# Converting a weight matrix in column parts: the first up projection of a fused HGRN2 and feed-forward kernel

## The chip, the cores and the metric

The kernel runs on one core of a Trainium2 chip. The metric is the device time of one execution in microseconds (us), lower is better. In the profile the engines are PE (TensorE: matmuls), DVE (VectorE), ACT (ScalarE), POOL (GpSimd) and SP (SyncE, which here only issues DMAs). Each engine runs its own instructions in order, and engines wait for each other on semaphores.

## The reference

An attention block without softmax (per batch, head and step a decayed outer-product state) is followed by a feed-forward block that multiplies two projections:

```python
f = 1.0 / (1.0 + np.exp(-f_logit))            # q, k, v, f_logit: (4, 8, 768, 48)
for t in range(S):
    state = f[:, :, t, :, None] * state + np.einsum('bhd,bhe->bhde', k[:, :, t], v[:, :, t])
    y[:, :, t] = np.einsum('bhd,bhde->bhe', q[:, :, t], state)
x = y.transpose(0, 2, 1, 3).reshape(3072, 384)
a = x @ w1                                    # w1, w2: (384, 1024)
b = x @ w2
h = a * b @ w3                                # w3: (1024, 1024)
out = h @ w_out                               # w_out: (1024, 384)
```

q, k, v and f_logit come as 32-bit floats. The four weight matrices come as 64-bit floats, and the kernel converts them to 32 bits on the chip.

## The kernel before, in words

**Chunks and blocks.** The 4 x 768 steps are 24 chunks (u = 0 to 23) of 128 steps, all 8 heads together. For each chunk DVE makes the running products of the gates by two scans (L531 forward, L553 backward) and from them Q (L547) and K (L561). PE multiplies them (L586, copied to SBUF by ACT at L709), POOL masks the result (L715), and PE makes the chunk's values in one visit (L660, L679). From chunk 4 on such a visit also begins the next chunk (L586 and L692), so the visit of chunk u needs K of chunk u+1 turned. Chunk 0 to 4 are turned by four PE transposes (L600) into a PSUM bank and a copy by ACT (L756). From chunk 5 on it is done without PE: ACT splits K into 16-bit halves (L732), a transposing DMA on SP's queue moves them (L735), ACT merges them (L740). The test for it is in `turning`, L750.

The values go to DRAM (`written`, L896, SP's queue) and come back in the layout of the projections (`gathered`, L899, POOL's queue). Four chunks make a block of 512 steps for the feed-forward part.

**Feed-forward.** Block 0 uses plain products (`part`, L950): a visit `up(jc, which)` multiplies 256 steps by 128 columns jc of w1 (which = 0) or w2 (which = 1) as three matmuls over the 384 rows (L928), each of which the profile shows as two instructions. ACT copies the w1 result (L965), DVE multiplies it by the w2 result (L970). There are 8 column groups jc, and the half of a matrix is jc // 4. Later blocks use products with fewer multiplications (L1024, L1179). w3 and w_out are first multiplied into one matrix wc by PE ("folds", L1496), which is then used by the down projection (`down`).

**Conversion of the weights.** `fetch` loads raw 64-bit words into a buffer in `place`. Per load, ACT turns the low words into something that can be joined (L1432). Then three DVE instructions make 32-bit floats: `shifted` (L1447), `signed` (L1451, the last reader of the raw buffer) and `joined` (L1457). w1 and w2 are four items of 384 rows by 512 columns, called A (w1, columns 0 to 511), B (w2, the same columns), C (w1, columns 512 to 1023) and D (w2, the same). An item has three loads, and 3 x 512 = 1536 elements per partition. D's raw words go to the same place as A's.

**Order.** Nothing is ordered by hand. All work is entered into `Plan` as tasks with an engine, an estimated cost, what they depend on, and a priority. `listed` simulates the engines and takes at each step the task that can start first, by priority if several can. The tasks are then emitted in that order, which fixes the order on every engine; the semaphore waits follow from what the instructions read and write. So a changed cost or priority may move instructions anywhere in the program. DMAs are tasks of a queue and of a pretended engine with a latency (`moves`). In the first stage the DVE work is also held in a fixed order, `"23ACBD"`: the scans and products of chunks 2 and 3, then the items. Up to planned time 130 (`FULL`), gaps that the plan sees on PE are filled with matmuls on a constant tile (`idle`, L408):

```python
for t in plan.order():
    if t["eng"] == "PE" and t["at"] < FULL:
        n = int((t["at"] - ready_at) / 0.43)
        if ready_at and n:
            idle(n)
        ready_at = t["end"]
```

Of the kernel before, what the change touches and what calls it, by code (L numbers as in the profile page):

```python
# [37 lines left out]
I32 = mybir.dt.int32  # L38
U32 = mybir.dt.uint32
U16 = mybir.dt.uint16  # L40
ALU = mybir.AluOpType
# [3 lines left out]
B, H, S, D = 4, 8, 768, 48  # L45
# [11 lines left out]
UB = TB // C  # L57
# [9 lines left out]
KH = KF // 2  # L67
# [12 lines left out]
SURE_W = 2.0  # L80
SURE_K = 1.0
SURE_Z = 0.8
WITH_DMA = 1.2
NEED = (0.0, 1.0, 2.0, 3.0)
DUE = (5.0, 8.0, 24.0, 26.0)
EARLY = "23ACBD"
# [212 lines left out]
def ranged(ctx, tc, q, k, f_logit, v, w1, w2, w3, w_out, out, ident, w12, wc, left):  # L299

    nc = tc.nc
# [72 lines left out]
    plan = Plan()  # L374
# [86 lines left out]
    tk = [{} for _ in range(NU)]  # L461

    def need(u):
        return NEED[u] if u < 4 else 60 + 14.5 * (u - 4)

    def turn_of(item):

# [5 lines left out]
    def moves(n, size, rate, emit, deps, prio, late=0.0, since=0.0, lanes=("lane",), issue=0.45, eng="SP"):  # L473


        for j in range(n):
            i = plan.add(eng, issue, (lambda: None) if j else emit, [d] if j else deps, prio - j * 1e-3, takes=lanes, lag=0.85, since=since)
            d = i
            t = plan.add("DMA", size / n / rate, lambda: None, [i], prio - j * 1e-3, lag=1.1 + late, frees=[i])
        return t  # L480
# [266 lines left out]
    def turning(u):  # L747

        s, t = st[u], tk[u]
        if u > 4:  # L750
            crossing(u)
            return

        def turned():
            s["kt"] = work.tile([P, HP, R], F32, name="kt")
            nc.scalar.copy(s["kt"].rearrange("p (b two) r -> p b (two r)", two=2), s["pk"])  # L756

        if u < NPE:
            t["t"] = plan.add("PE", 0.45, lambda: turn(u), [t["k"]] + past(u, 1, "d"), need(u) - 999)
        else:  # L760
            t["t"] = plan.add("PE", 0.45, lambda: turn(u), [t["k"]], need(u) - 999, takes=["f"])
        t["e"] = plan.add(
            "ACT", 0.55, turned, [t["t"]] + past(u, 2, "s"), need(u), frees=[t["t"]] if u >= NPE else [],
        )
# [32 lines left out]
    def rest(u):  # L797
        s, t = st[u], tk[u]
        opens, closes = u % NCH == 0, u % NCH == NCH - 1
        n0 = need(u)  # L800
# [111 lines left out]
        if u < NPE:  # L912
            t["z"] = plan.add("PE", 1.6, moved, [t["y"]], n0 - 996, takes=["f"], frees=[moving])
            t["x"] = plan.add("ACT", 0.55, settled, [t["z"]] + before, n0 - 20, frees=[t["z"]])
        else:
            t["z"] = moves(2, 197, 300, written, [t["y"]], n0 - 100, 0.8)
            t["x"] = moves(1, 197, 250, gathered, [t["z"]] + before, n0 - 100, SURE_X, issue=WITH_DMA, eng="POOL")


# [13 lines left out]
    def ffn(n):  # L933
# [16 lines left out]
        def part(c0, c1, jcs):  # L950
            cols = slice(c0 * C, c1 * C)
            nt = (c1 - c0) * C
            cost = 6 * max(0.135, nt * 0.322 / 384)

            def up(jc, which):
                def emit():
                    s["pu", jc, which, c0] = bank()
                    three(
                        s["pu", jc, which, c0][:, 0:nt], [up_weights(w12, which, kc, jc) for kc in range(KM)],
                        [s["xt"][:, kc, cols] for kc in range(KM)],  # L960
                    )
                return emit

            def keep_a(jc):
                return lambda: nc.scalar.copy(a_b(jc)[:, cols], s["pu", jc, 0, c0][:, 0:nt])  # L965

            def times(jc):
                def emit():
                    ab = a_b(jc)[:, cols]
                    nc.vector.tensor_tensor(ab, s["pu", jc, 1, c0][:, 0:nt], ab, ALU.mult)  # L970
                return emit

            for jc in jcs:
                h = jc // KH
                x = [tk[n * UB + c]["x"] for c in range(c0, c1)]
                n0 = 100 * n + 50 + 10 * (jc >= KH)
                pa = plan.add("PE", cost, up(jc, 0), x + pieces[0, h], n0, takes=["f"])
                ka = takes_ab(jc, plan.add("ACT", 0.2 + nt * 0.28 / 384, keep_a(jc), [pa], -10, frees=[pa]))
                pb = plan.add("PE", cost, up(jc, 1), x + pieces[1, h] + [pa], n0 - 5, takes=["f"])
                kb = plan.add("DVE", 0.16 + nt * 0.4 / 384, times(jc), [pb, ka], -10, frees=[pb])  # L980
                s["up"] += [pa, pb]
                s["done"][place_of(jc) // KH].append(kb)
# [424 lines left out]

        return [g for a, m, gs in users if a < where + n and where < a + m for g in gs]

    def fetch(loads_, where, prio, due, dst, waits=(), deps=()):  # L1410

        total = sum(n for _, n, _ in loads_)
        if not wide:
# [27 lines left out]
        spot[0] = (a0 + (total + 511) // 512 * 512) % 2048  # L1441
        m = magnitudes[:, a0 : a0 + total]
        mine = range(a0 // 512, (a0 + total + 511) // 512)
        s = {}

        def shifted():
            nc.vector.tensor_scalar(m.bitcast(U32), hi, 3, None, ALU.logical_shift_left)  # L1447

        def signed():
            s["to"] = dst()  # L1450
            nc.vector.scalar_tensor_tensor(  # L1451
                s["to"].bitcast(U32), hi, 0x80000000, lo, ALU.bitwise_and, ALU.bitwise_or
            )

        def joined():
            to = s["to"].bitcast(I32)
            nc.vector.tensor_tensor(to, m.bitcast(I32), to, ALU.add)  # L1457

        past = [joins[i] for i in mine if i in joins]
        h = plan.add("DVE", 0.16 + 0.27 * w, shifted, landed + past, due, shared=True)  # L1460
        g = plan.add("DVE", 0.16 + 0.53 * w, signed, [*low, h] + list(waits), due)
        j = plan.add("DVE", 0.16 + 0.53 * w, joined, [h, g], due - 1, shared=True)
        parts.append((g, j))
        joins.update({i: j for i in mine})
        got.append(g)
        return [j]

    def weights():
        due = dict(zip(((0, 0), (1, 0), (0, 1), (1, 1)), DUE))
        for item in (x for x in EARLY if x in "ABCD"):  # L1470
            half, which = divmod("ABCD".index(item), 2)
            w = (w1, w2)[which]
            cols = slice(half * KH * P, (half + 1) * KH * P)
            pieces[which, half] = fetch(
                [(kc * KH * P, KH * P, w[kc * P : kc * P + P, cols].unsqueeze(1)) for kc in range(KM)],
                EARLY_AT[item], turn_of(item), due[which, half],
                lambda which=which, half=half: w12[:, which, half].rearrange("p k c -> p (k c)"),
            )

    def folding():  # L1480
# [138 lines left out]
    for u in range(NU):  # L1619
# [26 lines left out]
            judged = plan.add("DVE", 0.2, decided, [moves(1, 0.4, 250, heard, [sent], 0, SPREAD)], -20)  # L1646
        if u % UB == UB - 1:
            ffn(u // UB)
    first, last = {}, {}
    for item in EARLY:  # L1650
        if item in "ABCD":
            half, which = divmod("ABCD".index(item), 2)
            mine = pieces[which, half]
            first[item], last[item] = [j["deps"][0] for j in mine], mine
        else:
            t = tk[int(item)]
            first[item], last[item] = [t["p"]], [t["q"], t["k"]]
    for a, b in zip("1" + EARLY, EARLY):
        for t in first[b]:
            t["deps"] += last[a] if a != "1" else [tk[1]["q"], tk[1]["k"]]  # L1660
    ready_at = 0.0
    for t in plan.order():
        if t["eng"] == "PE" and t["at"] < FULL:
# [383 lines left out]
```

## Time and profile before

| what | value |
|---|---|
| median of 3 runs | 452.43 us (452.41 to 453.13) |
| profiled execution | 452.64 us, span 450.9 us |
| TensorE clock granted, mean | 0.998 |
| PE busy | 442.3 us, 98% of the span |
| DVE busy | 357.1 us, 79% |
| ACT busy | 253.6 us, 56% |
| POOL busy | 96.0 us, 21% |
| PE share of the chain that ended last | 95% |

The span is what the profiler saw from the first to the last instruction; the execution's own time has 1.7 us around it. "Busy" is time in which an engine had an instruction running; the filler matmuls count as busy. The chain is followed back from the last instruction, at each step to what released it. In rows of instructions in order of time, the first number is the start and the second the duration in us, "x8" is how many were merged, and brackets give the idle time of the engine before the row and what ended it. In rows of groups, the numbers after the bar are busy us in total and mean ns of one.

### The profile page before, as it was taken

The page shows a single profiled execution, that of the slowest core. Times are in us where ns is not written, and L with a number is a line of the kernel's source. Part 1 is how long each engine was busy: PE and PEld are TensorE (multiplying, and loading weights), DVE is VectorE, ACT ScalarE, POOL GpSimd, SP SyncE. Part 2 cuts the span into 40 slices and gives each one's busy share as a digit, 9 for nine tenths or more (in the row PEclk, how much of TensorE's full clock was granted, in tenths as well). Part 3 has the DMA queues.
Part 4 walks back from the last instruction along what each step waited for, and adds up shares of the span by engine and source line. Part 5 has one row for each costly group of instructions (what it writes and reads, how often), then busy time and mean ns, then how long its engine had stood idle before and what let it go on. Part 6 is the DMA issues. An engine that isn't in the chain of part 4 may idle for free.

```text
span 450.9 us, 11720 instructions
## 1 busy us (share of the span) xinstructions
PE 442.3 (98%) x4720; PEld 386.2 (86%) x4720; DVE 357.1 (79%) x615; ACT 253.6 (56%) x559; POOL 96.0 (21%) x132
## 2 busy tenths in 40 slices
PE   7999999999999999999999999999999999999995
PEld 6788885566899888889988889998899988889995
DVE  8999998999898978998889958965669557667541
ACT  4576245554546768676676346656666656666100
POOL 9551003133432344344333102000020000000000
PEclk9999999999999999999999999999999999999999
DMA  6998699784566786677653156563264612331111
GB/s 177 265 401 252 251 319 318 206 201 125 127 146 173 204 184 161 141 176 194 168 145 87 27 160 218 175 206 100 93 197 154 213 47 93 94 94 48 36 71 39
DMA packets 51949, 73.10 MB, mean 162 GB/s; under 512 B 22849, under 2 KB 35010, under 8 KB 50866
## 3 DMA queue, kind: packets, MB, share of 16 engines
q1 hardware_dynamic: 49202, 64.05, 48.3%
q0 software_dynamic: 2688, 8.26, 6.4%
q8 instruction: 38, 0.62, 0.6%
q14 instruction: 21, 0.17, 0.1%
HBM read 58.88 MB, written 9.04 MB: 151 GB/s over the span
## 4 chain that ended last, share of the span: by engine, by line
PE 95%; DVE 1%; SPq 1%; DMA 1%; issue 0%; POOL 0%; POOLq 0%; DVEq 0%
PE f L928 29%; PE f L1024 17%; PE l L1179 13%; PE f L1179 10%; PE f L1496 9%; PE l L928 5%; PE py L660 3%; PE pa L586 2%; PE py L679 2%; PE pa L692 2%; SPq L497 1%; PE f L408 1%; DMA ab<-in_k_dram 1%; PE l L1024 1%; DVE K L561 0%
## 5 line engine op out<-in xcount | busy, mean ns | idle before, releaser
L715 POOL TENSOR_SCALAR_AFFINE_SELECT A<-A 64x512 f32<-64x512 f32 (+1 forms) x46 | 47.7, 1037 | 45.3 <-ACT A L709 43.1
L928 PE MATMUL f<-place 128*128 128x192 f32 x240 | 42.4, 327 | 0.0
L928 PE MATMUL f<-xt,w 128*128 128x256 f32 x192 | 42.3, 380 | 0.0
L1496 PE MATMUL f<-place 128*128 128x384 f32 x128 | 42.2, 489 | 0.0
L928 PEld LDWEIGHTS f<-xt,w 128*128 128x128 f32 x192 | 36.2, 190 | 4.9
L928 PEld LDWEIGHTS f<-place 128*128 128x128 f32 x240 | 39.6, 190 | 0.2
L1024 PE MATMUL f<-xt,w 128*128 128x256 f32 x156 | 39.2, 379 | 0.0
L1496 PEld LDWEIGHTS f<-place 128*128 128x128 f32 x128 | 24.1, 190 | 16.1
L899 POOL DMA_DIRECT2D xt<-yt x22 | 16.8, 765 | 96.9 <-PE l L1179 52.3
L1024 PEld LDWEIGHTS f<-xt,w 128*128 128x128 f32 x156 | 29.6, 190 | 4.0
L531 DVE TENSOR_TENSOR_SCAN fwd<-gate,floor 112x512 f32<-112x512 f32 x24 | 30.3, 1263 | 1.0 <-ACT gate L523 0.2
L553 DVE TENSOR_TENSOR_SCAN bwd<-gate,back 112x512 f32<-112x512 f32 x24 | 29.7, 1236 | 0.7
L740 ACT COPY kt<-halves 128x896 uint16<-128x896 uint16 x19 | 22.9, 1205 | 4.7 <-DMA halves<-A 4.7
L1024 PE MATMUL f<-place 128*128 128x256 f32 x92 | 24.9, 388 | 0.0
L1432 ACT ACTIVATE place<-place 128x512 f32<-128x512 uint32 (+2 forms) x24 | 21.3, 891 | 4.8 <-DMA place<-in_w_dram 2.7
L875 ACT ACTIVATE ys<-py 112x512 f32<-112x512 f32 x22 | 13.1, 596 | 19.1 <-PE py L679 19.1
L928 PE MATMUL f<-wc,ab 128*128 128x192 f32 x128 | 23.7, 329 | 0.1
L732 ACT COPY A<-K 112x1024 uint16<-112x1024 uint16 x19 | 19.8, 1042 | 3.8 <-DVE K L561 3.8
L928 PEld LDWEIGHTS f<-wc,ab 128*128 128x128 f32 x128 | 21.2, 190 | 0.7 <-PE f L408 0.5
L523 ACT ACTIVATE gate<-f 112x512 f32<-112x512 f32 x22 | 13.9, 633 | 12.6 <-DMA f<-in_f_logit_dram 7.8
L838 POOL TENSOR_TENSOR G<-lasts,gate 112x4 f32<-112x4 f32 x20 | 9.6, 479 | 52.3 <-ACT gate L523 26.8
L515 POOL DMA_DIRECT2D vt<-in_v_dram x20 | 11.5, 575 | 40.5 <-PE py L660 35.3
(292 smaller groups left out, 1061.8 us busy)
## 6 DMA issues: line engine op xcount, KB each, us to landing
place<-in_w_dram SPq DMA_DIRECT2D x21, 512.0 KB, 6.9
A<-in_w_dram SPq DMA_DIRECT2D x19, 512.0 KB, 3.8
place<-in_w_dram SPq DMA_DIRECT2D x8, 1024.0 KB, 6.6
q<-in_q_dram SPq DMA_DIRECT2D x46, 96.0 KB, 2.9
out_dram<-o SPq DMA_DIRECT2D x23, 192.0 KB, 2.7
k<-in_k_dram SPq DMA_DIRECT2D x44, 96.0 KB, 2.8
yt<-ys SPq DMA_DIRECT2D x44, 96.0 KB, 2.9
xt<-yt POOLq DMA_DIRECT2D x22, 192.0 KB, 4.1
```

The costliest lines, as they stand in the source:

```text
L523: nc.scalar.activation(gate[u % 2][:, 0:NQ], fu, AF.Sigmoid)
L531: nc.vector.tensor_tensor_scan(s["P"], gate[u % 2][:, 0:NQ], floor, 0.0, ALU.mult, ALU.max)
L553: nc.vector.tensor_tensor_scan(s["R"][:, ::-1], gate[u % 2][:, NQ:0:-1], back[:, ::-1], 0.0, ALU.mult, ALU.max)
L715: nc.gpsimd.affine_select(out=a, in_=a, pattern=pattern, compare_op=ALU.is_ge, fill=0.0, base=0, channel_multiplier=-1,)
L732: nc.scalar.copy(apart.rearrange("p (two n) -> p two n", two=2), s["K"].bitcast(U16).rearrange("p (n two) -> p two n", two=2))
L740: nc.scalar.copy(to, halves.rearrange("p (two n) -> p two n", two=2))
L899: nc.gpsimd.dma_start(block_xt()[:, :, cols], s["yt"].rearrange("(k p) c -> p k c", p=P))
L928: nc.tensor.matmul(out_, lhsT=lhs[i], rhs=rhs[i], start=start and i == 0, stop=i == len(lhs) - 1, skip_group_check=True,)
L1024: nc.tensor.matmul(q[nm][:, which * TH : which * TH + TH], lhsT=lhs[i](which), rhs=rhs[i], start=start and which == 0 and i == 0, stop=i = ...
L1179: nc.tensor.matmul(banks[g, c][:, which * TH : which * TH + TH], lhsT=lhs, rhs=x_node(a), start=first and which == 0, stop=True, skip_grou ...
L1432: nc.scalar.activation(part_.bitcast(F32), part_, AF.Copy, bias=2.0, scale=2.0**-51)
L1496: nc.tensor.matmul(w3s["p", jc], lhsT=w3s[jc][:, kc * P : kc * P + P], rhs=wos[:, kc], start=(kc == 0), stop=(kc == KF - 1),)
```

## The change

Six things change, all in what is entered into the plan:

- `fetch` can cut the conversion of an item into column parts. A and C (`CUT`) are cut in two parts of 256 columns each: three rows of 256 elements per part, with three DVE instructions each, instead of three instructions over 1536 elements. The loads and ACT's part stay whole.
- A visit of columns jc depends on the parts up to its own columns (the first two jc of a half on the first part, the other two on both).
- The fixed order of the first stage names the parts (`TURNS`).
- The plan counts a raw buffer as read when the joins have ended, and no longer when `signed` has ended.
- Chunk 5 is turned by PE as chunks 0 to 4 are (`u > 5`).
- Three numbers of the plan: the cost of a DMA issue on POOL (1.2 to 0.8), the spacing of the chunks' priorities (14.5 to 14.0), and an added delay in the plan after the write of the values, 0.8 to 3.0 for the chunks that are not the last of their block.

```diff
-WITH_DMA = 1.2
+CUT = "AC"
+TURNS = ('2', '3', 'A0', 'A1', 'C0', 'C1', 'B', 'D')
+WITH_DMA = 0.8
...
-        return NEED[u] if u < 4 else 60 + 14.5 * (u - 4)
+        return NEED[u] if u < 4 else 60 + 14.0 * (u - 4)
...
-        if u > 4:
+        if u > 5:
             crossing(u)
...
-            t["z"] = moves(2, 197, 300, written, [t["y"]], n0 - 100, 0.8)
+            t["z"] = moves(2, 197, 300, written, [t["y"]], n0 - 100, 0.8 if u % UB == UB - 1 else 3.0)
...
-                pa = plan.add("PE", cost, up(jc, 0), x + pieces[0, h], n0, takes=["f"])
+                pa = plan.add("PE", cost, up(jc, 0), x + pieces[0, h][: jc % KH * len(pieces[0, h]) // KH + 1], n0, takes=["f"])
...
-                pb = plan.add("PE", cost, up(jc, 1), x + pieces[1, h] + [pa], n0 - 5, takes=["f"])
+                pb = plan.add("PE", cost, up(jc, 1), x + pieces[1, h][: jc % KH * len(pieces[1, h]) // KH + 1] + [pa], n0 - 5, takes=["f"])
...
+        for c in range(cuts):
+            def of(t, c=c):
+                t = t.rearrange("p (k n) -> p k n", k=len(loads_))
+                return t[:, :, c * t.shape[2] // cuts : (c + 1) * t.shape[2] // cuts] if cuts > 1 else t
...
+            at_once = due + 0.1 * c
+            h = plan.add("DVE", 0.16 + 0.27 * w / cuts, shifted, landed + past, at_once, shared=True)
+            g = low if by_act else [plan.add("DVE", 0.16 + 0.53 * w / cuts, signed, [*low, h, *waits], at_once)]
+            j = plan.add("DVE", 0.16 + 0.53 * w / cuts, joined, [h, *g, *waits], at_once - 1, shared=True)
+            parts.append((h, j))
+            ended.append(j)
...
-        got.append(g)
-        return [j]
+        got += ended
+        return ended
...
+                cuts=2 if item in CUT else 1,
```

More of the change, by code (lines that the diff above doesn't have):

```diff
@@ L1408, in holders, with fetch @@
         return [g for a, m, gs in users if a < where + n and where < a + m for g in gs]
-    def fetch(loads_, where, prio, due, dst, waits=(), deps=()):
+    def fetch(loads_, where, prio, due, dst, waits=(), deps=(), by_act=False, cuts=1):
         total = sum(n for _, n, _ in loads_)
@@ L1443, in fetch @@
         mine = range(a0 // 512, (a0 + total + 511) // 512)
[L1444 to L1457, printed above, removed]
@@ L1459, in fetch, with shifted, whole, signed @@
-        past = [joins[i] for i in mine if i in joins]
[L1460 to L1463, printed above, removed]
+        past = [joins[i] for i in mine if i in joins]
+        ended = []
+        for c in range(cuts):
+            def of(t, c=c):
+                t = t.rearrange("p (k n) -> p k n", k=len(loads_))
+                return t[:, :, c * t.shape[2] // cuts : (c + 1) * t.shape[2] // cuts] if cuts > 1 else t
+            mc = m[:, c * total // cuts : (c + 1) * total // cuts]
+            mc = mc.rearrange("p (k n) -> p k n", k=len(loads_)) if cuts > 1 else mc
+            def shifted(of=of, mc=mc):
+                nc.vector.tensor_scalar(mc.bitcast(U32), of(hi), 3, None, ALU.logical_shift_left)
+            def whole(of=of):
+                return of(lo) if by_act else of(dst().bitcast(U32))
+            def signed(of=of, whole=whole):
+                nc.vector.scalar_tensor_tensor(whole(), of(hi), 0x80000000, of(lo), ALU.bitwise_and, ALU.bitwise_or)
+            def joined(of=of, mc=mc, whole=whole):
+                nc.vector.tensor_tensor(of(dst().bitcast(I32)), mc.bitcast(I32), whole().bitcast(I32), ALU.add)
+            at_once = due + 0.1 * c
[4 more added lines that the diff above has]
+            ended.append(j)
@@ L1648, in ranged @@
             ffn(u // UB)
[L1649 to L1654, printed above, removed]
+    chain = [(tk[1]["p"], [tk[1]["q"], tk[1]["k"]])]
+    for item in TURNS:
+        if item[0] in "ABCD":
+            half, which = divmod("ABCD".index(item[0]), 2)
+            js = pieces[which, half] if len(item) == 1 else [pieces[which, half][int(item[1])]]
+            chain.append((js[0]["deps"][0], js))
         else:
             t = tk[int(item)]
[L1657 to L1660, printed above, removed]
+            chain.append((t["p"], [t["q"], t["k"]]))
+    for (_, before), (t, _) in zip(chain, chain[1:]):
+        t["deps"] += before
     ready_at = 0.0
```

## The prediction

> **What bounds the kernel now.** I read the page first (busy times, the chain that ended last), then the waits of PE, then PE in order of time, to find where PE does nothing of use.
>
> ```profile
> span 450.9 us, 11720 instructions
> ...
> PE 442.3 (98%) x4720; PEld 386.2 (86%) x4720; DVE 357.1 (79%) x615; ACT 253.6 (56%) x559; POOL 96.0 (21%) x132
> ...
> PE 95%; DVE 1%; SPq 1%; DMA 1%; issue 0%; POOL 0%; POOLq 0%; DVEq 0%
> ```
>
> PE is busy 98% of the span and makes 95% of the chain. So the time is PE's work plus what PE loses, and another engine matters only where it makes PE wait. The waits of PE up to 130 us are four (total, times, longest):
>
> ```profile
> PE f L408 <- DVE floor L431: 1.8, 1, 1.8
> PE py L600 <- DVE K L561: 0.7, 1, 0.7
> PE f L600 <- DVE K L561: 0.5, 1, 0.5
> PE pa L692 <- issue: 0.5, 1, 0.5
> ```
>
> That is not all that PE loses. Where the planner expects a gap on PE it emits fillers (L408, a constant tile multiplied into a bank that nobody reads): a filler is a wait that looks busy. PE in order of time around the first up-projection visits (L928); start and duration come first:
>
> ```profile
> 24.90 1.89 PE L408 MATMUL f<-floor 112*128 112x256 f32 x8
> 26.72 1.00 PE L660 MATMUL py<-A,vt 64*64 64x64 f32 x32
> ...
> 29.66 0.70 PE L408 MATMUL f<-floor 112*128 112x256 f32 x2
> 30.20 4.05 PE L928 MATMUL f<-xt,w 128*128 128x256 f32 x18
> ...
> 35.56 26.17 PE L928 MATMUL f<-xt,w 128*128 128x256 f32 x120
> 61.56 0.55 PE L600 MATMUL f<-ident,K 112*128 112x112 f32 x4
> 61.95 5.36 PE L928 MATMUL f<-xt,w 128*128 128x256 f32 x24
> ```
>
> Ahead of the first L928, PE fills from 24.90 to 26.72, runs the visit of chunk 2, fills again from 29.66 to 30.20, and starts. From there no wait of PE stands in the list, and 120 matmuls in 26.17 us are 0.218 us each, against 5.36/24 = 0.223 in the short group: no hidden stall. A visit is six of them, 1.31 us. The one later loss, and the end:
>
> ```profile
> 122.10 0.60 PE L408 MATMUL f<-floor 112*128 112x256 f32 x2
> 122.76 1.57 PE L928 MATMUL f<-wc,ab 128*128 128x192 f32 x8
> ...
> 444.80 1.46 PE L928 MATMUL f<-wc,place 128*128 128x192 f32 x8
> ```
>
> So from 30.20 to 446.3 PE does work that stays, but for one pair of fillers (122.76 - 122.10 = 0.66).
>
> **The cut of A and C.** DVE converts the first half of w1 (A, 24.22 to 29.62), then the second (C, from 29.96), then B from 35.40; the rows from 55.77 are a w_out piece, of exactly the size of the new parts (768 elements):
>
> ```profile
> 24.22 1.28 DVE L1447 TENSOR_SCALAR place<-place 128x1536 uint32<-128x1536 uint32 x1 [0.61 <-DMA place<-in_w_dram]
> 25.42 0.34 DVE L788 TENSOR_TENSOR A<-pa,S 112x192 f32<-112x192 f32 x1
> ...
> 26.07 1.75 DVE L1451 SCALAR_TENSOR_TENSOR w<-place 128x1536 uint32<-128x1536 uint32 x1
> 27.86 1.76 DVE L1457 CUSTOM_DVE_ANT_0 w<-place,w 128x3072 uint16<-128x3072 uint16 x1
> 29.96 0.96 DVE L1447 TENSOR_SCALAR place<-place 128x1536 uint32<-128x1536 uint32 x1 [0.34 <-DMA place<-in_w_dram]
> ...
> 35.40 0.96 DVE L1447 TENSOR_SCALAR place<-place 128x1536 uint32<-128x1536 uint32 x1
> ...
> 39.86 0.96 DVE L1447 TENSOR_SCALAR place<-place 128x1536 uint32<-128x1536 uint32 x1
> ...
> 55.77 0.55 DVE L1447 TENSOR_SCALAR place<-place 128x768 uint32<-128x768 uint32 x1
> 56.23 0.95 DVE L1451 SCALAR_TENSOR_TENSOR place<-place 128x768 uint32<-128x768 uint32 x1
> ...
> 58.09 0.42 DVE L970 TENSOR_TENSOR ab<-f,ab 128x256 f32<-128x256 f32 x1
> ```
>
> A's data land just before 24.22 (DVE sat 0.61 us for them), and the cut doesn't move that. Today A is whole at 27.86 + 1.76 = 29.62. A part of 768 elements takes 58.09 - 55.77 = 2.32 us from start to start; with the state update of chunk 2 in between (26.07 - 25.42 = 0.65) the first part, A0, is done at 24.22 + 2.32 + 0.65 = 27.2, which is 2.4 earlier. But PE works in order and is in chunk 2's visit until 29.66, so only 30.20 - 29.66 = **0.54 us** of the 2.4 reaches the path: the second pair of fillers. A1 ends at 27.2 + 2.32 = 29.5 and is first needed two visits on, at 29.66 + 2 x 1.31 = 32.3. C's data land at 29.96 (DVE sat 0.34), so C starts as before.
>
> Uncut, an item takes 39.86 - 35.40 = 4.46 us; cut, 2 x 2.32 = 4.64. The six added instructions cost DVE 2 x 0.18 = 0.36 us. The 0.34 that DVE sat ahead of C covers A's share; C's 0.18 is passed on to B and D, where it counts below. The new parts are three rows of 256 and not one run of 768, a shape that no row shows: I take the 768 row as the nearest, with 0 to 0.2 us an item on top as the bound.
>
> [...]
>
> **The loads behind the cut.** D (second half of w2) loads into A's raw buffer, when the second of A's three instructions is through:
>
> ```profile
> 27.85 0.80 SPq L1428 DMA_DIRECT2D place<-in_w_dram  x2
> SPq L1428 <- DVE w L1451: 3.7, 1, 3.7
> ```
>
> SP stood 3.7 us for it. In a part it ends 56.23 + 0.95 - 55.77 = 1.41 after the start, so for A1 at 27.2 + 1.41 = 28.6: D's first two issues move 0.8 later, or behind chunk 2's yt writes if the planner, which now counts the buffer as free after the join alone, sorts them so. Queued behind on SP are yt, D's third load and the inputs of chunk 4. When D is needed:
>
> ```profile
> 41.25 1.76 DVE L1451 SCALAR_TENSOR_TENSOR w<-place 128x1536 uint32<-128x1536 uint32 x1 [0.43 <-ACT place L1432]
> ...
> 44.06 0.40 DVE L970 TENSOR_TENSOR ab<-f,ab 128x256 f32<-128x256 f32 x1
> ...
> 45.27 1.75 DVE L1457 CUSTOM_DVE_ANT_0 w<-place,w 128x3072 uint16<-128x3072 uint16 x1
> ...
> 47.52 0.42 DVE L970 TENSOR_TENSOR ab<-f,ab 128x256 f32<-128x256 f32 x1 [0.17 <-PE f L928]
> ```
>
> D is whole at 45.27 + 1.75 = 47.02. The product at 47.52, for which DVE waited on PE, is the fourth of four from 44.06 on: PE ended the fourth and last w2 visit of B's columns at about 47.45 and took D from there. The slack is 0.43. PE now comes 0.54 earlier, and D may be 0.8 + 0.18 later. I take 0: between D's last two instructions (43.01 to 45.27) DVE did other work, so the join can move up, and PE has other visits to do first. Without that cover it costs 0.54 + 0.98 - 0.43 = 1.1 us.
>
> **Chunk 5 turned on PE.** It loses two ACT copies and a transposing DMA on SP, and gains four transposes on PE and one ACT copy:
>
> ```profile
> L740 ACT COPY kt<-halves 128x896 uint16<-128x896 uint16 x19 | 22.9, 1205 | 4.7 <-DMA halves<-A 4.7
> L732 ACT COPY A<-K 112x1024 uint16<-112x1024 uint16 x19 | 19.8, 1042 | 3.8 <-DVE K L561 3.8
> L756 ACT COPY kt<-f 128x448 f32<-128x448 f32 x3 | 1.6, 530 | 1.1 <-PE f L600 1.1
> ```
>
> ACT saves 1.205 + 1.042 - 0.530 = 1.7 us, off the path at 56% busy. PE pays 61.95 - 61.56 = **0.39 us** (chunk 4's transposes, start to start), on the path, as PE has nothing idle there. A new wait: PE, in order, stands for K of chunk 5 where ACT stood, and all of PE's work is queued behind. Chunk 4's transposes did so without a wait, so I take 0; the longest wait for K in the list, 0.7, is the upper end. What chunk 5 gains:
>
> ```profile
> 88.31 1.20 ACT L740 COPY kt<-halves 128x896 uint16<-128x896 uint16 x1
> 94.22 0.45 PE L660 MATMUL py<-A,vt 64*64 64x64 f32 x16
> ```
>
> The visit at 94.22, which also begins chunk 5, needs the copy that ended at 89.51. Without it the visits of chunks 4 and 5 can move up between the weight folds, which moves PE's work about and takes none away.
>
> **The constants.** The spacing of 14.0, the issue cost of 0.8 and the delay of 3.0 emit nothing; they reorder. After 30.20 a new order can win the 0.66 at 122.10 at most. Before, chunk 2's fillers could shrink: its mask on POOL ended at 26.02 and its visit began at 26.72.
>
> ```profile
> 24.04 1.98 POOL L715 TENSOR_SCALAR_AFFINE_SELECT A<-A 64x512 f32<-64x512 f32 x2 [2.03 <-ACT A L709]
> ```
>
> A new order can also lose a wait of PE of the kind listed, up to 0.7. I take 0; the ends are -0.66 - 0.70 and +0.7.
>
> **Sum.** -0.54 + 0.39 = -0.15 on the profiled execution's own 452.64 (the span of 450.9 and 1.74 around it) gives 452.49. That execution lies 0.21 above the median of 452.43 (three runs, 452.41 to 453.13), so beside the median the forecast is 452.3. A measurement of this kernel tells no less than about 0.2%, 0.9 us, from no change: 451.5 to 453.3 is the same.
>
> **The rivals.**
> *More fillers go.* For: DVE's state update of chunk 2 comes 0.4 earlier behind a shift of half the size, and chunk 4's and 5's visits can move to where PE fills. Against: the visit of chunk 2 waits for the mask, which doesn't move, and the pair at 122.10 stands between PE's last up visit and a sum that needs its product. The pair at 122 alone gone: 452.3 - 0.66 = 451.6; chunk 2's fillers too: 450.9.
> *D is late* (slower). The place is PE's fifth w2 visit at about 46.9, the price up to 1.1: 453.4. It decides as slower from the point at which D is whole 1.5 us after 47.02 with PE in front of it. For: the slack of 0.43, and SP blocked longer. Against: DVE's order can move, PE has other visits.
> *The cut does nothing.* If a visit waits for both parts, or the planner keeps the pair of fillers, the 0.54 stays and chunk 5's 0.39 is added: 452.8.
>
> **How the numbers follow.** As summed 0.46 (its own range 451.9 to 452.8, by the 0.2 an item and half of the pair at 122); more fillers go 0.28; D late, or another new wait of PE, 0.17; the cut does nothing 0.09. Faster is most of the second case and a little of the first: 0.28. Slower is most of the third, and a share for stalls from the new order that no row prices: 0.19. The same: 0.53. The range reaches from most of the fillers gone to D late with a little more: 451.1 to 453.7.
>
> **What would show it.** Right: four conversions of w at 768 elements, the first join ending near 27.2; the first L928 at 29.7 with no pair of fillers ahead of it; L740 and L732 once less, four more L600; no PE wait near 47. Wrong: PE waiting for DVE's w at 46 to 48 (D late); no L408 at 122 or fewer ahead of 26.7 (more fillers gone); the first L928 still at 30.2; or new fillers or waits of PE between 35 and 260, which would make the whole sum wrong.

## The result, and the profile after

The changed kernel takes 454.92 us (median of 14 runs, 453.93 to 457.09); the kernel before took 452.77 beside it (14 runs, 452.25 to 453.23). The ratio is 1.0053, 95% interval 1.0042 to 1.0064: slower by 0.5%, where no change was forecast, and above the range. The profiled execution took 455.35, 2.71 more than the one of before. Of the experiments below, one execution of e3 took 1637.56 us and is left out of its numbers. The page's first lines and its chain:

```profile
span 453.6 us, 11712 instructions
...
PE 444.2 (98%) x4722; PEld 386.7 (85%) x4722; DVE 358.3 (79%) x621; ACT 252.3 (56%) x558; POOL 93.4 (21%) x132
...
PE 84%; DVE 7%; DMA 3%; POOL 2%; issue 1%; ACT 1%; SPq 0%; POOLq 0%; ACTq 0%; DVEq 0%
```

PE's part of the chain fell from 95% to 84%: other engines now end waits of PE. PE's waits that were not there before (total, times, longest):

```profile
PE f L930 <- issue: 0.9, 1, 0.9
PE f L410 <- DVE ab L972: 0.6, 1, 0.6
...
PE f L930 <- DVE w L1466: 0.4, 1, 0.4
PE f L930 <- ACT place L1303: 0.3, 1, 0.3
```

Lines have moved: the visits L928 are now L930, the fillers L408 are L410, the product L970 is L972, the three conversion instructions L1457, L1463 and L1466, the merging copy L740 is L742, the transposing DMA L735 is L737, the gather L899 is L901. In the experiments some move by a few lines more.

**The first visits.** PE in order of time:

```profile
28.16 1.56 PE L930 MATMUL f<-xt,w 128*128 128x256 f32 x6
...
30.63 4.15 PE L930 MATMUL f<-xt,w 128*128 128x256 f32 x18
...
36.09 0.70 PE L930 MATMUL f<-xt,w 128*128 128x256 f32 x2
37.19 25.73 PE L930 MATMUL f<-xt,w 128*128 128x256 f32 x118 [0.40 <-DVE w L1466]
```

The filler pair is gone and the first visit starts at 28.16, ahead of chunk 3's products. At 36.09 PE has 24 of the matmuls behind it. Before, it had 18 at 35.56, and six more are 1.31: a lead of 0.78. Then it stands. Two matmuls on from 36.09 would be 36.53, the next start at 37.19: 0.66 of the 0.78 are given back, in a visit of C's first columns, at the end of C's second join. DVE:

```profile
24.20 0.95 DVE L1457 TENSOR_SCALAR place<-place 128x768 uint32<-128x768 uint32 x1 [0.53 <-DMA place<-in_w_dram]
...
29.75 0.96 DVE L1466 CUSTOM_DVE_ANT_0 w<-w,place 128x1536 uint16<-128x1536 uint16 x1 [0.35 <-PE f L930]
...
33.47 0.95 DVE L1466 CUSTOM_DVE_ANT_0 w<-w,place 128x1536 uint16<-128x1536 uint16 x1
...
36.18 0.96 DVE L1466 CUSTOM_DVE_ANT_0 w<-w,place 128x1536 uint16<-128x1536 uint16 x1
...
45.18 1.75 DVE L1466 CUSTOM_DVE_ANT_0 w<-place,w 128x3072 uint16<-128x3072 uint16 x1
```

C's first part was joined at 33.47 + 0.95 = 34.42, and PE waited until 37.14. A's second join, at 29.75, waited for PE to finish with A's first columns. The shift of three rows of 256 takes 0.95; the shift of one run of 768 took 0.55. D is whole at 46.93, where it was at 47.02.

**Chunk 5's turn** costs what was summed (85.39 - 85.01 = 0.38):

```profile
85.01 0.55 PE L602 MATMUL f<-ident,K 112*128 112x112 f32 x4
85.39 5.02 PE L1507 MATMUL f<-place 128*128 128x384 f32 x15
```

**From the up to the down projection.** PE, then ACT:

```profile
117.13 5.45 PE L930 MATMUL f<-xt,w 128*128 128x256 f32 x24
123.16 0.70 PE L410 MATMUL f<-floor 112*128 112x256 f32 x2 [0.59 <-DVE ab L972]
123.70 1.47 PE L930 MATMUL f<-wc,ab 128*128 128x192 f32 x8
125.00 1.46 PE L930 MATMUL f<-place 128*128 128x192 f32 x8
126.75 1.57 PE L930 MATMUL f<-wc,ab 128*128 128x192 f32 x8 [0.29 <-ACT place L1303]
...
125.32 1.21 ACT L742 COPY kt<-halves 128x896 uint16<-128x896 uint16 x1 [2.49 <-DMA halves<-A]
126.39 0.31 ACT L1303 COPY place<-f 128x192 f32<-128x192 f32 x1
```

24 matmuls from 117.13 end near 122.41, and the first product with wc starts at 123.70: 1.29 between them, 0.66 before. The filler itself waited 0.59, since it writes a bank that DVE (L972) was still reading. Then the third group waits for the copy L1303, which ACT, in order, held behind L742, and L742 stood 2.49 for a transposing DMA: 126.75 against 125.00 + 1.30, a loss of 0.45.

**At 211 to 216** PE loses 1.5 for which "issue" stands:

```profile
211.71 0.37 PE L662 MATMUL py<-A,vt 64*48 64x64 f32 x10 [0.21 <-issue]
...
213.56 0.92 PE L930 MATMUL f<-place 128*128 128x192 f32 x4
215.34 2.11 PE L930 MATMUL f<-place 128*128 128x192 f32 x12 [0.86 <-issue]
```

The visit that began at 211.16 ran until 213.56, 2.40 where others take 1.89, and about 1.0 is lost ahead of 215.34.

The account in this execution: -0.78 + 0.66 (first visits), +0.39 (turn), 1.29 - 0.66 = +0.63 and +0.45 (into the down projection), +1.5 (211 to 216), together +2.85 of the measured 2.71. The rest, -0.14, is spread.

### The profile page after: what moved, and what is told of

It is laid out like the page before. It is cut to its first block, busy times and chain, and to the rows that moved or that the text cites. A ratio compares the mean times of both kernels' runs of the same rounds, so it can differ in the third digit from the quotient of the medians.

```text
span 453.6 us, 11712 instructions
## 1 busy us (share of the span) xinstructions
PE 444.2 (98%) x4722; PEld 386.7 (85%) x4722; DVE 358.3 (79%) x621; ACT 252.3 (56%) x558; POOL 93.4 (21%) x132
## 4 chain that ended last, share of the span: by engine, by line
PE 84%; DVE 7%; DMA 3%; POOL 2%; issue 1%; ACT 1%; SPq 0%; POOLq 0%; ACTq 0%; DVEq 0%
PE f L930 26%; PE f L1026 16%; PE l L1181 14%; PE f L1181 9%; PE l L930 5%; PE f L1507 3%; PE py L662 3%; PE pa L588 2%; DMA halves<-A 2%; PE py L681 2%; PE pa L694 1%; DVE place L1540 1%; POOL ab L448 1%; DMA place<-in_w_dram 1%; PE l L1026 1%
## 5 line engine op out<-in xcount | busy, mean ns | idle before, releaser
L717 POOL TENSOR_SCALAR_AFFINE_SELECT A<-A 64x512 f32<-64x512 f32 (+1 forms) x46 | 43.5, 946 | 42.7 <-ACT A L711 40.4
L930 PE MATMUL f<-xt,w 128*128 128x256 f32 x192 | 43.2, 382 | 0.4 <-DVE w L1466 0.4
L930 PE MATMUL f<-place 128*128 128x192 f32 x232 | 42.2, 328 | 0.9 <-issue 0.9
L930 PEld LDWEIGHTS f<-xt,w 128*128 128x128 f32 x192 | 35.9, 190 | 5.7 <-DVE w L1466 0.8
L930 PEld LDWEIGHTS f<-place 128*128 128x128 f32 x232 | 38.2, 190 | 1.4 <-issue 1.0
L1507 PEld LDWEIGHTS f<-place 128*128 128x128 f32 x128 | 24.1, 190 | 16.1
L901 POOL DMA_DIRECT2D xt<-yt x22 | 16.8, 763 | 89.1 <-PE l L1181 51.4
L533 DVE TENSOR_TENSOR_SCAN fwd<-gate,floor 112x512 f32<-112x512 f32 x24 | 31.9, 1329 | 1.5 <-ACT gate L525 0.3
L1026 PEld LDWEIGHTS f<-xt,w 128*128 128x128 f32 x148 | 28.0, 190 | 3.8
L742 ACT COPY kt<-halves 128x896 uint16<-128x896 uint16 x18 | 21.7, 1204 | 12.2 <-DMA halves<-A 12.2
L930 PE MATMUL f<-wc,ab 128*128 128x192 f32 x144 | 26.7, 328 | 0.3 <-ACT place L1303 0.3
L930 PEld LDWEIGHTS f<-wc,ab 128*128 128x128 f32 x144 | 23.9, 190 | 0.9 <-ACT place L1303 0.6
L840 POOL TENSOR_TENSOR G<-lasts,gate 112x4 f32<-112x4 f32 x20 | 11.2, 558 | 59.3 <-ACT lasts L538 30.8
L850 ACT ACTIVATE S<-S,G 112x48 f32<-112x48 f32 x72 | 18.2, 326 | 5.7 <-DVE S L793 5.6
L662 PEld LDWEIGHTS py<-A,vt 64*64 64x64 f32 (+1 forms) x672 | 13.5, 127 | 7.8 <-issue 7.3
```

The lines of the kernel that those rows point to most:

```text
L533: nc.vector.tensor_tensor_scan(s["P"], gate[u % 2][:, 0:NQ], floor, 0.0, ALU.mult, ALU.max)
L662: done = nc.tensor.matmul(y_block(u, hp, par, half)[p0 : p0 + w], lhsT=s["v"][half * W : half * W + W, h * D : h * D + w], rhs=s["A"][half ...
L717: nc.gpsimd.affine_select(out=a, in_=a, pattern=pattern, compare_op=ALU.is_ge, fill=0.0, base=0, channel_multiplier=-1,)
L742: nc.scalar.copy(to, halves.rearrange("p (two n) -> p two n", two=2))
L850: nc.scalar.activation(s["S"][:, hp], s["S"][:, hp], AF.Copy, scale=s["G"][:, hp : hp + 1])
L901: nc.gpsimd.dma_start(block_xt()[:, :, cols], s["yt"].rearrange("(k p) c -> p k c", p=P))
```

## The experiments

Theory R (regions): a visit of C's first columns waits for both parts, since the parts interleave in w12. Theory S (shape): the shift loses its speed on three rows. Theory O (order): the re-sorted plan costs by itself. Theory D, which came up on the way: the transposing DMA lands late because a gather is in flight beside it. Rival to these: the cut or the turn costs by its own work. A ratio is the time over that of the kernel before, run beside it.

**Raw words by parts (e1).** A part's shift reads one run of 768; the loads write rows of 2 KB instead of 4 KB.

```diff
...
+                    to_ = raw.rearrange("p (s k m) -> p s k m", s=cuts, k=len(loads_))[:, :, at_ // n]
+                    nc.sync.dma_start(to_, src.bitcast(U32).rearrange("p a (s m) -> p (a s) m", s=cuts))
...
```

> Every instruction stands in the order of the changed kernel; only the raw words of A and C lie by parts, so that a part's shift reads one run of 768 elements and not three rows of 256. Theory S (the shape slows the shift, 0.95 us where 0.55 was expected): the four shifts take 0.55, DVE gains 4 x 0.40 = 1.6 us by 37 us, C's second join ends near 36 and not at 37.1, PE's wait of 0.40 for it goes, and so may the wait of 0.59 for the last product near 122; 0.6 to 1.2 us faster than the changed kernel, 453.7 to 454.3. Rival: the shift's duration is set by contention and not by the shape: shifts stay at 0.95, time 454.9.

457.09 (455.46 to 460.13), ratio 1.0111 (1.0086 to 1.0136). The shift fell to 0.56, so S holds. The gain missed, since the first of A's loads lands later; the last does not, as the first shift starts at 24.01 and in the changed kernel at 24.20. DVE, ACT and PE:

```profile
24.01 0.56 DVE L1468 TENSOR_SCALAR place<-place 128x768 uint32<-128x768 uint32 x1 [0.31 <-DMA place<-in_w_dram]
...
23.99 0.68 ACT L1440 ACTIVATE place<-place 128x512 f32<-128x512 uint32 x1 [3.46 <-DMA place<-in_w_dram]
...
25.29 1.60 PE L906 MATMUL f<-ys,ab 112*128 112x128 f32 x12 [1.49 <-ACT ys L877]
```

ACT stood 3.46 for A's low words, and the copy ys that PE needs stood behind.

**The same with w12 by parts (e2).** The raw words of B and D lie by parts here too, so their loads are also in rows of 2 KB.

```diff
-    w12 = const.tile([P, 2, 2, KM, KH * P], F32, name="w12")
+    w12 = const.tile([P, 2, 2, 2, KM, 2 * P], F32, name="w12")
...
```

> As the run before, and w1 and w2 also lie by parts in SBUF, so that the two parts of a half don't interleave. Theory R (a visit waits for, and holds up, the other part because the parts' address ranges overlap): beyond the run before, A's second join no longer waits for PE's first visit (0.35 in the changed kernel), and PE never stands for a join of w; by time 0 to 0.4 us below the run before, 453.5 to 454.2. Rival: the wait near 37 was a true one, for C's first part coming late: then it goes already with the faster shifts, and this run equals the run before to 0.2 us, with A's second join still standing for PE.

458.19 (457.3 to 458.42). A's second join no longer waits for PE (it starts at 31.45, right behind its `signed`, and PE's first visit at 32.16), as R says. The wait for ys costs still more: L906 waits 1.96, and its 12 matmuls then take 2.92, at a granted clock of 0.51, where they took 1.60 in e1.

**The changed kernel without the cut (e3)** and **with chunk 5 turned by the DMA (e4).**

```diff
-CUT = "AC"
+CUT = ""
...
-        if u > 5:
+        if u > 4:
```

> The changed kernel with nothing cut, everything else of the change in place; the plan is made anew. If the cut is what costs (theories R and S): back to 452.8 plus 0.39 for chunk 5's transposes, 453.0 to 453.4. If the rest of the change costs (theory O: the new order puts waits of PE at 122, 126 and 211 to 215, together 2.1 us): 454.5 or more.

> The changed kernel with chunk 5 turned by the transposing DMA as before; the plan is made anew. By my sum: 0.39 us faster than the changed kernel, 454.5, if the order behind stays as good or bad as it is. Theory O: the visits of chunks 4 to 6 go back, and the waits at 122 to 126 and 211 to 215 move or go, so anything from 452.8 to 455; which of these PE waits are listed tells it.

e3: 456.35 (456.06 to 456.89), ratio 1.0077: without the cut the rest of the change costs more, so the cut's own work isn't what makes the change slower. (The plan is made anew here, so this doesn't part the cut from the order.) e4: 455.03 (453.79 to 455.86), ratio 1.0042: the 0.39 on PE is not won back. Both have another order, and fillers in it that e3's PE even waits for:

```profile
123.54 1.56 PE L410 MATMUL f<-floor 112*128 112x256 f32 x6 [0.82 <-DVE ab L972]
```

**Each part alone.** e5 is the changed kernel with the old three numbers; e6, e7 and e8 are the kernel before with the cut, the turn or the numbers alone.

```diff
# e8 (e5 takes these three back)
-WITH_DMA = 1.2
+WITH_DMA = 0.8
-        return NEED[u] if u < 4 else 60 + 14.5 * (u - 4)
+        return NEED[u] if u < 4 else 60 + 14.0 * (u - 4)
-            t["z"] = moves(2, 197, 300, written, [t["y"]], n0 - 100, 0.8)
+            t["z"] = moves(2, 197, 300, written, [t["y"]], n0 - 100, 0.8 if u % UB == UB - 1 else 3.0)
# e7
-        if u > 4:
+        if u > 5:
# e6: CUT, TURNS and the visits' parts as in the change, but in fetch
-        got += ended
+            got += g
```

> The changed kernel with the three numbers of the order put back (spacing 14.5, issue cost 1.2, delay 0.8); the cut of A and C and chunk 5's turn on PE stay. If the three numbers bring the bad order (theory O: the filler held by VectorE's product near 123, the copy behind the late transposing DMA near 126, about 1.1 us, and with them the stalls near 212), it takes 452.8 to 453.8. If the loss is the cut's or the turn's own, or the stalls near 212 come whatever the order, it stays at 454.6 to 455.3. First L930 near 28.2 to 29.7 in both cases, and a wait for C's second join of 0.4 to 0.9.

> The kernel before with the cut of A and C alone: parts of 256 columns, visits that wait for the parts of their own columns, and the raw buffer still counted free after the instruction it was before; chunk 5 is turned by the DMA and the numbers are the old ones. By the prediction's own sum -0.54 against before: 452.2. By the theory that a visit of C's first columns waits for C's second join (0.5 to 0.6 lost again) no change: 452.5 to 453.0, with a wait of PE for the join near 36. If a reordering alone brings stalls and late copies, 453.5 to 455, with a filler or visit of more than 0.5 us too long between 115 and 225.

> The kernel before with chunk 5's transposes on PE alone, nothing cut, the old numbers. By the prediction's sum +0.39: 453.1. If the new order costs more than the work added (theory O), 453.6 to 455, with the excess in waits of PE between 85 and 225; if the early copy for chunk 5 lets visits move up, 452.1 to 452.7.

> The kernel before with the three numbers alone (spacing 14.0, issue cost 0.8, delay 3.0); no instruction is added or taken away. The prediction took 0, with ends of -1.36 and +0.7. Theory O, that the new order costs: 454.0 to 455.0, with the waits near 123 and 126 as in the changed kernel. If it takes the cut and the numbers together: 452.5 to 453.2.

e5: 459.47 (458.13 to 460.94), ratio 1.0152. e6: 453.76 (453.11 to 456.72), 1.0036. e7: 455.58 (454.78 to 457.89), 1.0073. e8: 455.75 (453.47 to 457.89), 1.0071. All are slower than before, and no sum of parts gives the whole: the numbers cost alone, and taking them out costs too. e8 adds and removes no instruction but fillers; it has three groups of them past 40, at 47.81, 123.03 and 131.51, with 0.43 + 1.09 + 0.43 of PE's time from start to start, where before has one of 0.66. Together that is 1.29 more, and e8's profiled execution (454.49) is 1.85 above before's; how much of the 1.29 PE could have used is not shown. The largest:

```profile
123.03 1.03 PE L408 MATMUL f<-floor 112*128 112x256 f32 x4
```

In e7 a part of the excess over the 0.39 is again ACT's queue behind a transposing DMA; ACT and PE:

```profile
169.64 1.23 ACT L740 COPY kt<-halves 128x896 uint16<-128x896 uint16 x1 [2.76 <-DMA halves<-A]
...
172.31 1.99 PE L1024 MATMUL f<-xt,place 128*128 128x256 f32 x8 [0.81 <-ACT place L1065]
```

So theory O holds in this form: each order has its own fillers and late copies, and six further orders (e3 to e8) were all slower than before's.

**The changed kernel once more (e9).**

> The changed kernel itself once more, for a second profiled execution. If the stalls of PE at 211 (0.51) and 215 (0.86, put down to issue) come by chance of the instruction fetch, they stand elsewhere, or have another size, in this profile, while the waits of the order stay where they were: the filler that waits for the product near 123 (0.59), the wait for ScalarE's copy near 126 (0.29), the wait for the conversion near 36 (0.40). If the stalls too are fixed by the order, they stand at 211 and 215 again with the same sizes. Time 454.9 as before, within 453.9 to 457.1.

455.34 (454.37 to 458.0); its profiled execution took 458.0. The waits near 36, 123 and 126 stand in their places. The stall at 215 has another size (0.28), and that at 211 is gone: the visit takes 1.89. So these two are not fixed by the order; whether the instruction fetch makes them, no run shows. The wait for the copy is 2.18 here and not 0.29, and after it PE runs the next visit at a granted clock of 0.54 (in the second fence the columns are the stretch, its length, the busy time of PE, PEld, DVE, ACT and POOL, the granted clock, the DMA share and GB/s):

```profile
128.66 1.76 PE L930 MATMUL f<-wc,ab 128*128 128x192 f32 x8 [2.18 <-ACT place L1303]
...
130.82 1.08 PE L588 MATMUL pa<-Q,K 48*64 48x64 f32 x32
```

```profile
130.30:133.60 3.30, 3.30 (x130) 3.19 (x129) 2.57 (x4) 2.12 (x4) 0.58 (x1) 0.54 0.17 50
133.60:137.00 3.40, 3.40 (x28) 3.40 (x22) 1.78 (x5) 0.92 (x4) 1.30 (x2) 1.00 0.90 229
```

The visit from 130.35 to 133.58 takes 3.23 and not 1.89. So the wait of 2.18 and the slow visit behind it cost 2.2 + 1.3 here, at a place whose wait was 0.29 in the other execution. Gaps of 2.18 and of 1.96 (e2) were followed by a granted clock of 0.54 and 0.51. After the gap of 1.43 in e10 it stayed at 1.00 (126 to 132), and after that of 1.49 in e1 the 12 matmuls took 1.60, where they take 1.52 in the changed kernel. At what length of a gap the clock falls is not shown; in e14 below it fell after shorter ones.

Why the DMA is late shows in its issues (start of the issue at the end of the row, then the time to landing), first after's transposing DMA and gather, then before's:

```profile
L737 SPq DMA_TRANSPOSE halves<-A x1: 1397/1397/1397, 117.5 to 117.5; - x1
DMA to landing us min/median/max: 7.8/7.8/7.8
L901 POOL DMA_DIRECT2D xt<-yt x1: 752/752/752, 117.5 to 117.5; - x1
DMA to landing us min/median/max: 7.6/7.6/7.6
```

```profile
L735 SPq DMA_TRANSPOSE halves<-A x1: 1222/1222/1222, 118.0 to 118.0; - x1
DMA to landing us min/median/max: 3.3/3.3/3.3
L899 POOL DMA_DIRECT2D xt<-yt x1: 779/779/779, 113.6 to 113.6; - x1
DMA to landing us min/median/max: 2.9/2.9/2.9
```

Before, the gather of xt went out on POOL at 113.6 and had landed; in the new order a load of vt stands ahead of it on POOL, the gather and the transposing DMA both go out at 117.5, and each takes more than twice its time. The second place looks the same: four gathers from 200.4, a transposing DMA issued at 202.5, its copy on ACT not before 211.40. This is theory D. A gather beside it is not enough, though: before has three gathers that go out within 0.5 us of a transposing DMA (near 102, 130 and 206), and there it lands after 4.1, 4.5 and 4.2. The slowest of the three, beside a gather of 130.1:

```profile
L735 SPq DMA_TRANSPOSE halves<-A x1: 1961/1961/1961, 130.6 to 130.6; - x1
DMA to landing us min/median/max: 4.5/4.5/4.5
```

At 117.5 the load of vt (issued at 116.96, landed 4.2 later) is in flight too. What it takes besides the gather was not tested.

**Without the late filler (e10).**

```diff
-FULL = 130.0
+FULL = 100.0
```

> The changed kernel without the one pair of fillers near 123; the order of all other instructions is the same. If the pair is what delays the first product of w_out with the folded weights (it waits for VectorE's last read of its bank, and then runs 0.54 ahead of useful work), the time falls by 0.4 to 0.6 against the changed kernel, to 454.4. If the product had to wait for VectorE's ab anyway, it stays within 0.1: a wait of PE in its place of about the same 0.6 to 1.1.

454.46 (453.19 to 456.07), ratio 1.0036 (1.0024 to 1.0048): about 0.5 to 0.9 under the two medians of the changed kernel. The intervals overlap (1.0042 to 1.0064 and, in e9, 1.0037 to 1.0063), so the gain is not sure, and in its profile a wait takes the filler's place and the late copy is still there:

```profile
124.79 1.57 PE L930 MATMUL f<-place 128*128 128x192 f32 x8 [0.74 <-DVE place L1296]
127.79 1.57 PE L930 MATMUL f<-wc,ab 128*128 128x192 f32 x8 [1.43 <-ACT place L1303]
```

**w12 by parts, loads as they were (e11).** The layout of w12 is e2's, the loads and raw words are the changed kernel's.

> The changed kernel with w12 laid out so that each part of 256 columns is one run of 768, in the same order; loads and raw words as in the changed kernel, so the shift keeps its three rows of 256 (0.95). The second halves of B and D are now two instructions each (four more on VectorE). By theory R (two parts that interleave in w12 count as one stretch of addresses): the wait of PE for C's second join near 36 to 37 and the wait of A1's join for PE's first visit go: 0.4 to 0.6 faster than the changed kernel, 454.4. If the wait is for anything else it stays near 37 and the time is the same or 0.3 more by the four instructions.

453.34 (452.68 to 456.2), ratio 1.002 (1.0007 to 1.0034): 1.6 to 2.0 under the two medians of the changed kernel, more than R's price. PE runs from 36.27 without a wait, and A's second join (29.21) follows its `signed` at once:

```profile
36.27 6.09 PE L930 MATMUL f<-xt,w 128*128 128x256 f32 x27
```

R holds, for the 0.66 of the profile. The two matmuls that ran at 36.09 in the changed kernel fit it: they are the visit's first product, whose columns lie ahead of everything that C's second part writes in w12; the second and third lie between its rows. The other 1 or so is not located by this run: in its profile PE waits 0.52 for the copy near 126 and loses nothing at 215.

**The cut alone, parts apart, no fillers after 40 (e12), and the same with its fillers (e15).**

> The cut alone on the kernel before (old numbers, chunk 5 by the DMA, the order of the run with the cut alone), with w12 laid out by parts as in the run before this, and no fillers after 40. Against the cut alone (453.76; its PE had 0.42 lost near 36, a filler of 0.43 at 41.8 and four of 1.09 at 122.2): if theory R and the fillers are what it lost, 0.4 + 0.4 + up to 0.5 go: 452.5 to 453.0, level with the kernel before at best 0.3 below it. If PE merely waits where it filled, only the 0.4 near 36: 453.3 to 453.6.

> The cut alone with the parts apart, as in the run of 452.32, but with the fillers after 40 left in. By theory R the layout alone wins 0.42 of the cut alone's 453.76, and the filler at 41.8 (0.43), which stood before a visit that needed nothing late, costs its full time, that at 122 its 1.09 less the 0.74 that PE waits without it: 452.32 + 0.43 + 0.35 = 453.1. If the fillers cost nothing (PE would have waited), 452.3 to 452.5.

e12: 452.32 (452.18 to 453.38), ratio 0.9992 (0.9983 to 1.0001), with 452.68 for the kernel before beside it. e15: 453.14 (452.71 to 453.87), ratio 1.0008. So from e6's 453.76 the layout wins 0.6 and the fillers' absence 0.8, as priced: the filler at 41.8 stood before a visit that waited for nothing. e12 is the best version here, 0.6% under the changed kernel and level with the kernel before.

**The gather away from the transposing DMA (e13), and with the parts apart as well (e14).**

```diff
         def gathered():
+            if u == 5:
+                return
+            if u == 6:
+                other = st[5]["yt"].rearrange("(k p) c -> p k c", p=P)
+                nc.gpsimd.dma_start(block_xt()[:, :, C : 2 * C], other)
```

> The changed kernel with chunk 5's gather of xt issued together with chunk 6's instead of near 117.5; every other instruction in the same order. If the gather in flight beside it is what makes the transposing DMA late (issued at 117.54, landed 7.8 later, against 3.3 in the kernel before), it lands about 3.5 after its issue, ScalarE's copies near 122 to 126 come without a wait, and PE's wait for the copy near 126 goes: 0.5 in the best runs of the changed kernel and 2 or more in the worst, so 454.0 to 454.5 in the median (454.9 and 455.3 before) and a narrower spread. If the DMA is late by itself, nothing changes: 454.9 to 455.4.

> The changed kernel with both repairs: w12 laid out by parts (453.34 alone) and chunk 5's gather of xt beside chunk 6's. If the two waits add up, 452.5 to 453.0: level with the kernel before, the early 0.5 to 0.9 won and chunk 5's 0.39 and the filler near 123 paid. If the late copy made little in that run, 453.2 to 453.5.

e13: 454.17 (453.1 to 454.47), ratio 1.0024 (1.0014 to 1.0035): 0.8 to 1.2 under the changed kernel, the upper end of its runs down from 457 or 458 to 454.5, as theory D asks. The gather now goes out at 120.42 and the load of vt where it did. ACT's merging copy no longer waits, and PE starts the third group at 126.22, 1.30 after the second (ACT, then PE):

```profile
122.65 1.19 ACT L742 COPY kt<-halves 128x896 uint16<-128x896 uint16 x1
...
126.22 1.46 PE L935 MATMUL f<-wc,ab 128*128 128x192 f32 x8
```

e14: 453.4 (452.73 to 456.78), ratio 1.0017: level with e11, so the two repairs did not add up. Its profiled execution (456.78) had the second place at its worst:

```profile
212.53 0.57 PE L694 MATMUL pa<-vt,kt 64*48 64x48 f32 x32 [0.82 <-ACT kt L742]
...
214.76 3.57 PE L935 MATMUL f<-place 128*128 128x192 f32 x11 [0.97 <-issue]
```

From 214.7 to 218.5 its granted clock was 0.55 (0.67 from 214 to 216, 0.50 from 216 to 218), after two gaps of 0.82 and 0.97.

**Both gathers away (e17), and the second one in e12 (e18).**

```diff
+            if u in (12, 13, 14, 15):
+                later.append(gather_now)
...
+            if u == 21:                       # e18: 22
+                for gather_now in later:
+                    gather_now()
```

> The changed kernel with the parts of the weights apart, chunk 5's gather of xt beside chunk 6's, and the four gathers of the block of chunks 12 to 15, which went out together near 200, after the mask of chunk 21 near 246; the order of everything else as in the changed kernel. If gathers in flight beside a transposing DMA are what stalls PE at both places, no wait for a copy near 126 or 212 and no gap in the visits at 210 to 216 is left, the spread shrinks to about 1 and the time falls from 453.4 to 452.6 to 453.0. If the stalls at 210 to 216 come from the instruction fetch by itself, they stay, and the time is 453.2 to 453.5.

> The version of 452.32 (the cut alone, parts apart, no fillers after 40) with the four gathers of chunks 12 to 15 after the mask of chunk 22: its transposing DMA at 202 had 5.4 us of packets beside them, and its PE lost 0.23 near 205. 452.0 to 452.2, which would be faster than the kernel before by 0.1%; 452.3 if PE had cover there.

e17: 461.2 (460.24 to 461.7); e18: 458.82 (458.31 to 460.92). Both missed by a mistake in the edit: some products read this xt before 246, and PE stood for it. Up to there e17 can be read. In the changed kernel and in e17, which share the order, the same visit begins at 236.48 and 233.69 (in e13 at 234.32):

```profile
236.48 0.45 PE L662 MATMUL py<-A,vt 64*64 64x64 f32 x16
```

```profile
233.69 0.45 PE L662 MATMUL py<-A,vt 64*64 64x64 f32 x16
...
245.44 2.04 PE L1197 MATMUL f<-xt,w 128*128 128x256 f32 x4 [5.28 <-DMA xt<-yt]
```

e17 is 2.79 ahead of the changed kernel there, with no wait near 126 and none between 210 and 216. That is as much as the whole loss (2.71). As a time it is an estimate, 455.35 - 2.79 = 452.6: a kernel with the gathers issued between 203 and 240 was not run. For e18 the question stays open.

How much of this the second move won is not shown. The transposing DMA near 202 landed 3.7 after its issue in e17 and 8.8 after it in the changed kernel, so theory D holds for the DMA. But e10, e11 and e13 have the four gathers where the changed kernel has them, ACT's copy waits there (1.95, 2.33 and 0.70), and PE loses at most 0.1 between 210 and 216 in their profiles too. e17's lead of 0.63 over e13 is what the layout won (0.66).

**Before without its pair of fillers (e16).**

```diff
-FULL = 130.0
+FULL = 100.0
```

> The kernel before without the pair of fillers at 122.10, its order as it is. The prediction priced the pair at 0.66 if it went: 452.0. From the changed kernel without its pair (a wait of 0.74 for VectorE's product took its place) at most 0.1 to 0.2 is won: 452.5 to 452.6.

452.58 (452.12 to 452.81), ratio 0.9992 (0.9983 to 1.0001): at most 0.2 of the 0.66.

## Why the prediction was wrong, step by step

- **First visits, -0.54.** The filler pair went, as said, and so did PE's gap of 0.46 for "issue" at 28.7: a lead of 0.78. The step then failed on a dependence that it took from the plan: the parts are apart there, and on the chip a visit of C's first columns waited for C's second join (0.66), until w12 was laid out by parts (e11, e12).
- **The cut's cost on DVE, 0.36 with a bound of 0.2 an item for the shape.** The bound failed. Three rows of 256 take 0.95 in the shift and one run 0.55 (e1: 0.56): 4 x 0.40 = 1.6 more on DVE. The 0.36 for the added instructions was not the term that mattered. What it is in the shape that costs the 0.40 the runs don't tell: no run here tried another number of rows.
- **D late.** It was not: whole at 46.93, though its loads went out from 29.95, behind chunk 2's yt writes, where the first two went out from 27.85 before. The cover named (DVE moves the join up) held.
- **Chunk 5, +0.39.** Right on the spot (0.38). But undoing it won nothing (e4) and doing it alone cost 2.9 (e7), since both re-sort the rest.
- **The constants, 0, with ends of -1.36 and +0.7.** This is the step that made the forecast wrong: it is the sum's only term for a new order, and it was put at nothing. Alone the constants cost 3.0 in the median (e8), and the new order of all changes together cost about 0.6 at the filler, 0.45 to 3.5 at the late copy, and up to 1.5 at 211 to 216. I bounded a new order by waits that PE had in the old one, as if a new wait could only be of a kind and size already seen. What the constants add to the new order when the cut and the turn are in it too, the runs don't tell: without them (e5) the time was 459.47.
- **The pair of fillers at 122, -0.66 if it goes.** Wrong as a price: e16 won 0.2 or less, though its first product with wc starts 0.56 earlier (122.20), and in e10 PE waits 0.74 where it filled. The filler at 41.8 in e6 was worth its full time. What a filler costs is what PE could have done in its place.
- **Rivals.** "More fillers go" did not happen; "the cut does nothing" is close to what the first visits came to (0.12 left of 0.78), by one of the two conditions that it named: a visit waited for both parts, here of C. "D late, or another new wait" had the right side and the wrong place. The share for "stalls from the new order that no row prices" was what happened, and too small.
- **What I could have seen.** That L740 heads ACT's queue with 4.7 of waits for the transposing DMA, in 3 of 19, stood in a row that I quoted, as something off the path. After, it is 12.2:

```profile
L742 ACT COPY kt<-halves 128x896 uint16<-128x896 uint16 x18 | 21.7, 1204 | 12.2 <-DMA halves<-A 12.2
```

Which of the changes put the gather beside the transposing DMA was not shown. How much the second late place costs in a typical run of e14, whose median is 0.8 above the estimate for e17, stays open too. So does "issue" at 215: it is gone in e17, but also in e10, e11 and e13, which have the gathers beside the transposing DMA, and what PE waited for in it no row names.

## What to carry to other kernels

Re-sorting this planned program had a price of its own, which no sum of the parts gave: seven orders of this work (after and e3 to e8) were 0.4 to 1.5% slower than the one before. That may also say that before's order is an unusually good one, which the runs can't tell. Either way, test a change with the order held, as e9 to e18 did. When an engine has a DMA wait in its queue, as ACT had with L742 (2.49), ask what useful copies stand behind it (here L1303, at 126.39, and at 125.12 in e13) and which other DMAs a new order can put in flight beside it. Parts that are to be waited for apart should lie apart in memory: interleaved in w12 they cost a visit 0.66, and laid out by parts (e11) PE ran on from 36.27 without a wait.

## What the runs showed that I had not expected

- A transposing DMA and a gather issued together at 117.5, with a load of vt just ahead, took 7.8 and 7.6 us to land. Before, issued 4.4 apart, they took 3.3 and 2.9, and three other pairs there, issued within 0.5, 4.1 to 4.5 and 3.1 to 4.0.
- PE's granted clock fell to 0.54 for 3.3 us after a gap of 2.18 us (e9) and to 0.51 after one of 1.96 (e2, 12 matmuls in 2.92); after 1.43 (e10) it was 1.00, and after 1.49 (e1) the same 12 matmuls took 1.60. Two gaps of 0.82 and 0.97 close together were followed by 0.55 (e14).
- The shift of 768 words takes 0.95 in three rows and 0.55 in one.
- Loads in rows of 2 KB in place of 4 KB put A's first words on ACT 3.3 us later (23.99 in e1, 20.68 in the changed kernel), though the last of A's words came no later.
